# Attention with two mixture layers on one core: maxima and subtractions first, a new start, gate constants in groups, chained weight decodes

## The chip, the core and the metric

The kernel runs on one core of a Trainium2 chip. A core has engines with queues of their own: TensorE (PE) multiplies matrices into PSUM banks, VectorE (DVE), ScalarE (ACT) and GpSimd (POOL) work on elements, SyncE (SP) issues most of the DMA transfers. Each engine runs its queue in order; an instruction that waits holds everything behind it on that engine. What is compared is the time of one launch in microseconds (us); lower is better.

## The reference

```
phi(x) = concat(exp(p), exp(-p)),  p = x @ w_phi - max|x @ w_phi|       # 64 -> 2 x 128 features
kv = phi(k)^T v;  z = sum phi(k)                                        # per batch and head
att = (phi(q) kv) / (phi(q) z + 1e-6)                                   # 8 batches, 8 heads, 576 tokens, 64
x = att as 4608 tokens x 512
h = x @ w_in;  x = (h * cos(h)) @ w_out                                 # first layer, 512 -> 2048 -> 512, float64 weights
logits = x @ w_gate + bias[modality]                                    # second layer: one of 8 experts for a token
out = gate * relu(x @ w1[e]) @ w2[e]                                    # 512 -> 1024 -> 512
```

## The kernel before

**Attention** goes by items: 16 of them, each two batches by two heads. An item's 576 tokens a batch are cut into five groups (`GR`: 2, 2, 1, 2 and 2 chunks), and the program has five steps m=0..4 per item, the one of m=2 with half the work. A step has two halves. `turns(j,m)` (L225) turns a part of the k and q of item j+1 with PE transposes (`pt`), which ACT copies to `kT` and `qT`; turns and exponentiates q features of two steps ago (`ptt`, ACT to `qx`); turns finished outputs (`po`, ACT to `xo`); and lets ACT exponentiate k features (`ke`). `products(j,m)` (L237) puts the projections of q and k into one PSUM tile `pj` (L124), the numerators of item j-1 into `pn` (L198), and `kv` (L162) of two steps ago. DVE then takes, for q and k, the maximum of absolute values (`m_q`, `m_k`, L129) and subtracts it (`t_q`, `t_k`, L130), and divides the numerators (`rd`, `xs`, L203 to L205). `pj` has one buffer (`bufs=1`), so the next step's `pj` starts when `t_k` of this step has read the last one. Nearly all of this is kept in program order.

**Decodes.** The weights of the first layer come as float64. Each of 32 pieces (512 KB) is loaded to a staging tile `st`, and `decoding` (L387) turns it into a pair of float32r tiles: Abs on ACT (L414), `min`, shift, two ORs on DVE (L415 to L418), a cast on ACT (L419), and a subtraction on POOL. In attention there is one staging tile (`sx`); `stage()` asks for the next load right after the second OR and the cast have been issued. The caller of `moes` walks attention by `next(att)`, two a step, and from n=32 on puts one of a decode's four parts (Abs and `min`; shift; first OR; second OR, cast, the next load and the subtraction) at every second n, from n%10==2 of an item; there are 12 such decodes (items 3 to 14), and more during the last 20 of the 170 half steps. The rest is decoded in the first steps of the first layer, one a step.

**Start.** The first k loads, then w_phi, then q and v loads of item 0, then the loads of item 1; five turns ahead of the first `pj`. After 15 half steps `gate_consts` (L266) issues the constants of the second layer's gate and of its routing in one lump, POOL fills a table and a block of zeros, and SP writes them.

**First layer** (`step(F)`): 9 blocks of 512 tokens by 16 pieces; L455 is its first matmul `ph`, and at F>=3 each step decodes one piece as long as any is left.

Of the kernel before, what the change touches and what calls it, by code (L numbers as in the profile page):

```python
# [264 lines left out]

def gate_consts(tc, ctx, cpool, ps, ident, modality_id, modality_bias, w_gate, wgt):  # L266
    nc=tc.nc
    C={}
    with tc.tile_pool(name="g_tmp",bufs=1) as tp:

        wgr=tp.tile([P,4,8],F32,name="wgr")
        nc.sync.dma_start(wgr,w_gate.rearrange("(c p) e -> p c e",p=P))
        pg=ps.tile([P,512],F32,tag="tr",name="pg")
        for c in range(4): nc.tensor.transpose(pg[0:8,c*P:(c+1)*P],wgr[:,c,:],ident)
        gt=tp.tile([8,512],F32,name="gt")
        nc.vector.tensor_copy(gt,pg[0:8,:])
        nc.sync.dma_start(wgt[:,:],gt)
        g1=cpool.tile([P,4,16],F32R,name="g1"); g2=cpool.tile([P,4,16],F32R,name="g2")
        nc.vector.tensor_copy(g1[:,:,0:8],wgr)
        nc.vector.tensor_tensor(g1[:,:,8:16],wgr,f32(g1[:,:,0:8]),ALU.subtract)  # L280
        nc.vector.tensor_copy(g2[:,:,0:8],wgr)
        nc.vector.memset(f32(g2[:,:,8:16]),0.0)

        fold=cpool.tile([16,8],F32,name="fold")
        nc.vector.tensor_tensor(fold,ident[0:16,0:8],ident[0:16,8:16],ALU.add)

        tf=tp.tile([P,P],F32,name="tf")
        nc.gpsimd.memset(tf,1.0)
        nc.gpsimd.affine_select(out=tf,in_=tf,compare_op=ALU.is_gt,fill=0.0,base=0,pattern=[[1,P]],channel_multiplier=-1)
        tri=cpool.tile([P,P],BF16,name="tri"); nc.vector.tensor_copy(tri,tf)  # L290
        one=cpool.tile([P,P],BF16,name="one"); nc.vector.memset(one,1.0)

        ri=tp.tile([P,8],I32,name="ri"); nc.gpsimd.iota(ri,pattern=[[-1,8]],base=8,channel_multiplier=0)
        rev=cpool.tile([P,8],F32,name="rev"); nc.vector.tensor_copy(rev,ri)

        rg=tp.tile([P,8],I32,name="rg"); nc.gpsimd.iota(rg,pattern=[[REG,8]],base=0,channel_multiplier=0)
        run=cpool.tile([P,8],F32,name="run0"); nc.vector.tensor_copy(run,rg)
        base=cpool.tile([P,8],F32,name="base"); nc.vector.tensor_copy(base,rg)
        nm=tp.tile([P,8],I32,name="nm"); nc.gpsimd.iota(nm,pattern=[[1,8]],base=0,channel_multiplier=0)
        num=cpool.tile([P,8],F32,name="num"); nc.vector.tensor_copy(num,nm)  # L300

        sl=tp.tile([1,25],I32,name="sl"); nc.gpsimd.iota(sl,pattern=[[1,25]],base=0,channel_multiplier=0)
        slot=cpool.tile([1,25],F32,name="slot"); nc.vector.tensor_copy(slot,sl)
        ones=cpool.tile([1,16],F32,name="ones"); nc.vector.memset(ones,1.0)

        tok=cpool.tile([P,4,9],I32,name="tok")
        nc.gpsimd.iota(tok[:,:,0:4],pattern=[[1152,4],[1,4]],base=0,channel_multiplier=4)
        nc.gpsimd.iota(tok[0:64,:,4:5],pattern=[[1152,4],[0,1]],base=512,channel_multiplier=1)
        nc.gpsimd.iota(tok[64:128,:,4:5],pattern=[[1152,4],[0,1]],base=1088,channel_multiplier=1)
        nc.gpsimd.iota(tok[:,:,5:9],pattern=[[1152,4],[1,4]],base=576,channel_multiplier=4)  # L310

        mi=tp.tile([P,4,9,2],I32,name="mi")
        ms=modality_id.bitcast(I32).rearrange("(a t w) -> a t w",a=4,w=2)
        for b,c0 in ((0,0),(1,5)):
            nc.sync.dma_start(mi[:,:,c0:c0+4,:].rearrange("p a c w -> p a (c w)"),ms[:,576*b:576*b+512,:].rearrange("a (p c) w -> p a (c w)",c=4))
            nc.sync.dma_start(mi[64*b:64*b+64,:,4,:],ms[:,576*b+512:576*b+576,:].rearrange("a p w -> p a w"))
        mf=tp.tile([P,36],F32,name="mf"); nc.vector.tensor_copy(mf,mi[:,:,:,0].rearrange("p a c -> p (a c)"))
        mz=tp.tile([P,36],F32,name="mz"); nc.vector.tensor_scalar(mz,mf,-1.0,1.0,op0=ALU.mult,op1=ALU.add)
        mb=tp.tile([P,2,8],F32,name="mb")
        nc.sync.dma_start(mb.rearrange("p a e -> p (a e)"),modality_bias.rearrange("(o a) e -> o (a e)",o=1).to_broadcast([P,16]))  # L320
        bt=cpool.tile([P,36,8],F32,name="bt"); b0=tp.tile([P,36,8],F32,name="b0")
        nc.vector.tensor_tensor(bt,mf.unsqueeze(2).to_broadcast([P,36,8]),mb[:,1:2,:].to_broadcast([P,36,8]),ALU.mult)
        nc.vector.tensor_tensor(b0,mz.unsqueeze(2).to_broadcast([P,36,8]),mb[:,0:1,:].to_broadcast([P,36,8]),ALU.mult)
        nc.vector.tensor_tensor(bt,bt,b0,ALU.add)
    C.update(g1=g1,g2=g2,fold=fold,tri=tri,one=one,rev=rev,run=run,base=base,tok=tok,bt=bt,num=num,slot=slot,ones=ones,pool=cpool)
    return C
# [597 lines left out]
def kernel(  # L924
# [28 lines left out]
    def consts():  # L953
        with tc.tile_pool(name="fill", bufs=1) as tp:
# [10 lines left out]
        return gate_consts(tc, ctx, cpool, ps, ident, modality_id, modality_bias, w_gate, wgt)

# [39 lines left out]
```

## Time and profile before

| | |
|---|---|
| time, median of 3 runs | 1710.75 us (1710.69 to 1710.86) |
| the profiled execution | 1708.39 us, span 1706.3 us |
| granted PE clock, mean | 0.987 of full speed |
| busy: PE, weight loads, DVE, ACT, POOL | 95%, 81%, 67%, 49%, 25% |
| attention, first to last `pj` | 11.96 to 373.73 us |

The span runs from the first to the last instruction of the profiled execution; the time is that of the whole launch. Attention ends near 400 us, the first layer near 1200 us, the rest is the second layer.

### The profile page before, as it was taken

Reading aid. Unit: us, or ns where it says so; the run is one execution under the profiler, and the core shown is the slowest. Engines: PE = TensorE matmul, PEld = TensorE weight load, DVE = VectorE, ACT = ScalarE, POOL = GpSimd, SP = SyncE. Lnnn points to the kernel's source line nnn. Section 1 sums busy time; section 2 is a strip of 40 time slices with the busy share of each in tenths; the row PEclk is TensorE's granted clock in tenths of the full one; section 3 lists DMA queues with packets and bytes.
Section 4 is the critical chain, followed back from the end, with each engine's and each line's share of the span. In section 5 each row is a group of like instructions: output and inputs, shape, how many; then the busy total and the mean of one; then the engine's idle time right before and its main releaser. Section 6 shows DMA issues by size and latency. Waiting matters only on the chain.

```text
span 1706.3 us, 33457 instructions
## 1 busy us (share of the span) xinstructions
PE 1618.9 (95%) x13058; PEld 1384.3 (81%) x13058; DVE 1145.9 (67%) x2332; ACT 829.2 (49%) x1529; POOL 427.7 (25%) x351
## 2 busy tenths in 40 slices
PE   6999999989899999999999999999789999999987
PEld 5888888877678888888888888888679999999976
DVE  4677777787885868676777777754556565665545
ACT  4566666655443434343433334343445555655545
POOL 0000000023232433334333333343222112211111
PEclk8999999999999999999999999999899999999999
DMA  6344444423220101010000101001378666767656
GB/s 186 100 134 126 129 137 135 128 91 121 87 99 13 38 13 37 13 37 14 26 25 7 43 7 38 7 7 36 126 240 305 218 219 228 252 210 224 226 167 205
DMA packets 142544, 190.05 MB, mean 111 GB/s; under 512 B 64536, under 2 KB 89240, under 8 KB 142371
## 3 DMA queue, kind: packets, MB, share of 16 engines
q1 hardware_dynamic: 134578, 166.74, 31.0%
q0 software_dynamic: 7792, 21.02, 3.7%
q8 instruction: 107, 1.75, 0.4%
q14 instruction: 67, 0.54, 0.1%
HBM read 157.98 MB, written 30.51 MB: 110 GB/s over the span
## 4 chain that ended last, share of the span: by engine, by line
PE 72%; DVE 13%; issue 5%; DMA 5%; ACT 4%; SPq 1%; POOL 1%; another core or an unknown queue 0%; DVEq 0%; POOLq 0%; ACTq 0%
PE ph L455 19%; PE acc L489 15%; PE mh L739 11%; PE po L751 10%; PE acc L494 4%; PE pj L124 3%; PE kv L162 3%; PE pn L198 2%; DMA tab<-rec,pi 2%; PE pt L109 2%; DVE x L445 1%; DMA raw<-in_moe_w_dram 1%; DVE t_k L130 1%; DVE d_t L406 1%; DVE m_k L129 1%
## 5 line engine op out<-in xcount | busy, mean ns | idle before, releaser
L455 PE MATMUL ph<-x,w 128*128 128x512 f32 x1728 | 424.8, 393 | 9.0 <-DVE fr L475 4.5
L455 PEld LDWEIGHTS ph<-x,w 128*128 128x128 f32 x1728 | 322.7, 188 | 85.7 <-DVE fr L475 7.4
L478 POOL TENSOR_TENSOR gl<-fr,gh 128x512 fp32r<-128x512 f32 x144 | 217.9, 1515 | 437.3 <-DVE gh L477 378.9
L699 DVE TENSOR_TENSOR m<-raw,m 128x512 fp32r<-128x512 f32 x320 | 210.2, 694 | 142.8 <-ACT m L698 142.7
L489 PE MATMUL acc<-w,gh 128*128 128x512 f32 x896 | 276.9, 390 | 1.0 <-DVE w L410 0.6
L698 ACT CAST m<-raw 128x512 fp32r<-128x512 f32 x320 | 187.0, 618 | 68.0 <-PE mh L739 33.6
L739 PEld LDWEIGHTS mh<-xT,m 128*128 128x128 f32 x1728 | 211.2, 193 | 6.3 <-DVE hl L742 2.8
L739 PE MATMUL mh<-xT,m 128*128 128x256 f32 x1728 | 212.3, 284 | 4.0 <-DVE hl L742 2.6
L468 ACT ACTIVATE n<-ph 128x512 int32<-128x512 f32 x144 | 85.8, 596 | 256.3 <-PE ph L455 256.2
L489 PEld LDWEIGHTS acc<-w,gh 128*128 128x128 f32 x896 | 168.2, 188 | 37.5 <-DVE w L410 1.9
L470 DVE SCALAR_TENSOR_TENSOR fr<-ph,n 128x512 f32<-128x512 f32 x144 | 99.2, 689 | 141.7 <-ACT n L468 127.9
L519 DVE SCALAR_TENSOR_TENSOR junk<-x1T,wg 128x512 f32<-128x512 f32 x224 | 183.3, 818 | 0.0
L751 PE MATMUL po<-m,hh 128*128 128x512 f32 x576 | 180.1, 394 | 1.8 <-ACT hh L741 1.8
L489 PE MATMUL acc<-w,gl 128*128 128x512 f32 x448 | 174.4, 389 | 0.0
L472 ACT ACTIVATE fr<-fr 128x512 f32<-128x512 f32 x144 | 91.1, 633 | 153.1 <-DVE fr L470 152.3
L475 DVE SCALAR_TENSOR_TENSOR fr<-fr,ph 128x512 f32<-128x512 f32 x144 | 98.7, 685 | 68.5 <-ACT fr L473 68.4
L751 PEld LDWEIGHTS po<-m,hh 128*128 128x128 f32 x576 | 105.3, 188 | 22.0 <-ACT hh L741 2.3
...
L751 PE MATMUL po<-m,hl 128*128 128x512 f32 x288 | 112.4, 390 | 0.1
L129 DVE TENSOR_REDUCE m_q<-pj 128x4 f32<-128x512 f32 (+1 forms) x80 | 51.0, 638 | 84.6 <-PE pj L124 84.5
L489 PEld LDWEIGHTS acc<-w,gl 128*128 128x128 f32 x448 | 84.1, 188 | 17.4
L473 ACT ACTIVATE fr<-fr 128x512 f32<-128x512 f32 x144 | 91.0, 632 | 4.3
(195 smaller groups left out, 2365.0 us busy)
## 6 DMA issues: line engine op xcount, KB each, us to landing
...
```

The costliest lines, as they stand in the source:

```text
L455: nc.tensor.matmul(ph,A[:,ws],xhl[u,d][k],start=n[0]==0,stop=n[0]==11); n[0]+=1
L470: nc.vector.scalar_tensor_tensor(g,ph,INV2PI,n,op0=ALU.mult,op1=ALU.subtract)
L472: nc.scalar.activation(g,g,AF.Sin,scale=math.pi)
L473: nc.scalar.activation(g,g,AF.Square)
L475: nc.vector.scalar_tensor_tensor(g,g,-0.5,ph,op0=ALU.add,op1=ALU.mult)
L478: nc.gpsimd.tensor_tensor(gl,g,f32(gh),ALU.subtract)
L489: nc.tensor.matmul(accs[u][c],A[:,ws],B,start=(f==0 and k==0),stop=(f==NF-1 and k==2))
L519: return lambda: tc.keep_in_program_order(nc.vector.scalar_tensor_tensor(junk,x1T[u,c],1.0,wg[e],op0=ALU.mult,op1=ALU.mult,accum_out=lgs[u ...
L698: keep(nc.scalar.copy(h,a))
L699: keep(nc.vector.tensor_tensor(l,a,f32(h),ALU.subtract))
L739: nc.tensor.matmul(ph[:,f2*T:(f2+1)*T],A[:,ws],B[d//2][:,xs],start=n==0,stop=n==11); n+=1
L751: nc.tensor.matmul(po[c],A[:,ws],B,start=(f==0 and j==0),stop=(f==NF2-1 and j==2))
```

## The change

In each step DVE takes both maxima and both subtractions before it divides the numerators, and the 64-wide `kv` of m=4 is issued behind `pj` instead of ahead of it. The first loads are k and q of both batches, then w_phi, then the small remainders; only the turns of m=0 and m=3 stand ahead of the first `pj`, and the others are spread by `FIRST`. Matmuls on a tile of zeros (`warm`) are put at the start (6) and in the steps of item 0 (3). `gate_consts` is a generator whose groups come at n=9, 17, 19, 21, 23 and 25. The stepped decodes become 14; they are chained, so that the last part of one and the first of the next come in one call, and a part is taken at four of the ten half steps of an item, from n=10. Two more tiles take decoded weights during attention (`xw`, 6 for 4), two fewer later (`wl`, 12 for 14).

```diff
-    ld("k",0)
-    for s in range(2): nc.sync.dma_start(w2[s*D:(s+1)*D,:],w_phi)
-    ld("q",0); ld("v",0)
+    load_first()
+    ld("v",0)
     for t in "kqv": ld(t,1)
-    for m in range(5): turn(0,m)()
+    warm(6)
+    for m in (0,3): turn(0,m)()
...
+    FIRST=((),((0,2),),((0,1),(0,4)),((1,0),(1,1)),((1,2),(1,3)))
...
-        for n in ((),(0,),(1,),(2,3),(4,))[m] if j==0 else (m,) if j+1<NI else (): vecs.append(turn(j+1,n))
+        for i,n in FIRST[m] if j==0 else ((1,4),(2,0)) if j==1 and m==0 else ((j+1,m),):
+            if i<NI: vecs.append(turn(i,n))
...
+        vecs=proj(j,m) if j<NI else []
         if todo and g==2: kv(i,g)
-        vq=vk=vn=None
-        if j<NI: vq,vk=proj(j,m)
-        if 0<=j-1<NI: vn=num(j-1,m)
+        if 0<=j-1<NI: vecs.append(num(j-1,m))
+        elif m<4: warm(3)
         if todo and g!=2: kv(i,g)
-        if vq: vq()
-        if vn: vn()
+        for f in vecs: f()
         if todo and g==2: kvfin(i,0)
         if todo and g==4: kvfin(i,1)
-        if vk: vk()
...
-    for _ in range(15): next(att)
-    C=consts()
-    stage()
-    for n in range(15,170-TAIL):
+    setup=consts()
+    work=itertools.chain.from_iterable(decoding(steps=True) for _ in range(14))
+    for n in range(170-TAIL):
         next(att)
-
-        if n%10==2 and 3<=n//10<15: work=decoding(steps=True)
-        if n>=32 and n%2==0: next(work,None)
+        if n==8: stage()
+        if n==9: next(setup)
+        if n in (17,19,21,23): C=next(setup)
+        if n==25:
+            for _ in setup: pass
+        if 10<=n and n%10 in (0,2,4,6): next(work,None)
+    for _ in work: pass
...
-    early=["wx"]*5+["qe"]*3+["xw"]*4+["xT"]*4+["raw_q","sx"]
+    early=["wx"]*5+["qe"]*3+["xw"]*6+["xT"]*4+["raw_q","sx"]
```

How the engines' queues change is shown at three places. The number in a name such as `m_q_1` is the step m; the last number only tells tiles apart.

DVE, a step m=1 of a middle item, in the kernel before (L415 is the `min` of a decode, L416 its shift, L168 copies `kv` to `kvz`):

```order
L129 TENSOR_REDUCE m_q_1_1771<-pj_1_1726 128x4
L130 TENSOR_TENSOR t_q_1_1731<-pj_1_1726,m_q_1_1771 128x512
L415 TENSOR_SCALAR d_t_1_1722<-d_t_1_1722 128x512
L203 TENSOR_SCALAR rd_1_1774<-pn_1_1737 128x4
L129 TENSOR_REDUCE m_k_1_1780<-pj_1_1726 128x4
L204 RECIPROCAL rd_1_1774<-rd_1_1774 128x4
L168 COPY kvz_1_1778<-kv_1_1562 128x260
L205 TENSOR_TENSOR xs_1_1754<-pn_1_1737,rd_1_1774 128x256
L130 TENSOR_TENSOR t_k_1_1736<-pj_1_1726,m_k_1_1780 128x512
L416 TENSOR_SCALAR d_t_1_1722<-d_t_1_1722 128x512
```

Here `t_k` stands behind the division and the copy. DVE, the same step in the changed kernel, from the last operation of one decode (L435, the second OR) to the `min` (L432) and shift (L433) of the next:

```order
L435 SCALAR_TENSOR_TENSOR d_t_2_1068<-st_0_1065,d_t_2_1068 128x512
L141 TENSOR_REDUCE m_q_1_1428<-pj_1_1383 128x4
L142 TENSOR_TENSOR t_q_1_1388<-pj_1_1383,m_q_1_1428 128x512
L141 TENSOR_REDUCE m_k_1_1431<-pj_1_1383 128x4
L215 TENSOR_SCALAR rd_1_1434<-pn_1_1394 128x4
L142 TENSOR_TENSOR t_k_1_1393<-pj_1_1383,m_k_1_1431 128x512
L216 RECIPROCAL rd_1_1434<-rd_1_1434 128x4
L180 COPY kvz_1_1438<-kv_1_1224 128x260
L432 TENSOR_SCALAR d_t_3_1379<-d_t_3_1379 128x512
L217 TENSOR_TENSOR xs_1_1411<-pn_1_1394,rd_1_1434 128x256
L433 TENSOR_SCALAR d_t_3_1379<-d_t_3_1379 128x512
```

`t_k` now stands ahead of the division's last steps and of the copy, and the next decode's `min` follows the last decode's second OR by one step. ACT in the kernel before, where a decode begins: its Abs (L414) stands behind the exponentials of a step, far from the cast (L419) of the decode before, two steps and more earlier:

```order
L419 CAST w_0_1326<-d_t_0_1325 128x512
L112 COPY kT_1612<-pt_0_1611 128x512
L183 ACTIVATE qx_3_1622<-ptt_3_1617 128x2x256 x2
L216 COPY xo_1396<-po_3_1623 128x256
L141 ACTIVATE ke_4_1630<-t_k_4_1580 128x4x128
L142 ACTIVATE ke_4_1630<-t_k_4_1580 128x4x128
L112 COPY kT_1612<-pt_1_1688 128x512
L183 ACTIVATE qx_4_1698<-ptt_4_1693 128x2x256 x2
L216 COPY xo_1396<-po_4_1699 128x256
L141 ACTIVATE ke_0_1707<-t_k_0_1643 128x4x128
L142 ACTIVATE ke_0_1707<-t_k_0_1643 128x4x128
L414 ACTIVATE d_t_1_1722<-st_0_1558 128x512
```

The same place on ACT in the changed kernel (L436 the cast, L431 the next Abs, L124 copies of turned k and q):

```order
L153 ACTIVATE ke_0_1359<-t_k_0_1295 128x4x128
L154 ACTIVATE ke_0_1359<-t_k_0_1295 128x4x128
L436 CAST w_2_1069<-d_t_2_1068 128x512
L431 ACTIVATE d_t_3_1379<-st_0_1376 128x512
L124 COPY kT_1263<-pt_2_1440 128x128
L124 COPY qT_1442<-pt_2_1440 128x128
L195 ACTIVATE qx_0_1449<-ptt_0_1444 128x2x256 x2
L228 COPY xo_1450<-po_0_1451 128x256
```

The Abs now stands right behind the cast, and the copies of the next turn behind the Abs. Last, DVE where item 1 begins, in the kernel before (`rev` and `run` are constants from POOL):

```order
L129 TENSOR_REDUCE m_k_4_361<-pj_4_345 128x4
L130 TENSOR_TENSOR t_k_4_355<-pj_4_345,m_k_4_361 128x512
L129 TENSOR_REDUCE m_q_0_427<-pj_0_382 128x4
L294 CAST rev<-ri 128x8
L297 CAST run_602<-rg 128x8
L130 TENSOR_TENSOR t_q_0_387<-pj_0_382,m_q_0_427 128x512
```

and in the changed kernel (`mf` is a cast of the loaded modality numbers `mi`):

```order
L141 TENSOR_REDUCE m_k_4_380<-pj_4_357 128x4
L180 COPY kvz_0_383<-kv_0_250 128x260
L142 TENSOR_TENSOR t_k_4_367<-pj_4_357,m_k_4_380 128x512
L286 CAST mf<-mi 128x36
L286 TENSOR_SCALAR mz<-mf 128x36
L141 TENSOR_REDUCE m_q_0_497<-pj_0_452 128x4
L432 TENSOR_SCALAR d_t_0_448<-d_t_0_448 128x512
L142 TENSOR_TENSOR t_q_0_457<-pj_0_452,m_q_0_497 128x512
```

`rev` and `run` stand ahead of the first step of all now; `mf` and `mz` stand ahead of `m_q` of item 1, and the first decode's `min` behind it.

## Rows read from the trace of the kernel before

**Rows 1.** Busy time of each engine, 200 to 220 us: us and instructions, clock, DMA share.

```profile
200.00:220.00 20.00, 17.95 (x352) 16.15 (x351) 14.68 (x37) 14.32 (x33) 1.41 (x2) 1.00 0.49 147
```

**Rows 2.** Waits, 60 to 340 us: engine, waiting line, releaser: total, times, longest.

```profile
PE pj L124 <- DVE t_k L130: 24.6, 25, 1.3
```

**Rows 3.** Timeline, PE: start, us, line, operation, tiles, in brackets the idle before.

```profile
200.29 0.71 PE L124 MATMUL pj<-w,qT 64*128 64x128 f32 x8
...
205.80 0.49 PE L124 MATMUL pj<-w,qT 64*128 64x128 f32 x4 [1.31 <-DVE t_k L130]
...
209.24 0.71 PE L124 MATMUL pj<-w,qT 64*128 64x128 f32 x8
...
213.26 1.11 PE L162 MATMUL kv<-v,ke 64*128 64x65 f32 x16
214.21 0.67 PE L124 MATMUL pj<-w,qT 64*128 64x128 f32 x8
...
218.39 0.72 PE L124 MATMUL pj<-w,qT 64*128 64x128 f32 x8 [0.74 <-DVE t_k L130]
...
222.74 0.71 PE L124 MATMUL pj<-w,qT 64*128 64x128 f32 x8
```

**Rows 4.** Timeline, DVE, steps m=4 and m=0 of the same item.

```profile
217.55 0.69 DVE L130 TENSOR_TENSOR t_k<-pj,m_k 128x512 f32<-128x512 f32 x1
...
219.59 0.69 DVE L129 TENSOR_REDUCE m_q<-pj 128x4 f32<-128x512 f32 x1 [1.01 <-PE pj L124]
```

**Rows 5.** Groups of DVE by shape, 60 to 340 us: busy, mean ns, idle before.

```profile
L129 DVE TENSOR_REDUCE m_q<-pj 128x2 f32<-128x256 f32 x12 | 5.1, 425 | 7.1 <-PE pj L124 7.1
```

**Rows 6.** The staging tile, 60 to 340 us; one decode's load, Abs and `min`.

```profile
DMA to landing us min/median/max: 3.7/4.7/6.3
...
214.25 0.34 SPq L380 DMA_DIRECT2D st<-in_moe_w_out_dram  x1
...
224.94 0.70 ACT L414 ACTIVATE d_t<-st 128x512 f32<-128x512 f32 x1
...
225.68 0.43 DVE L415 TENSOR_SCALAR d_t<-d_t 128x512 f32<-128x512 f32 x1 [0.32 <-ACT d_t L414]
```

**Rows 7.** Timeline of the start: PE, DVE and SP.

```profile
34.28 0.72 PE L124 MATMUL pj<-w,qT 64*128 64x128 f32 x8 [1.97 <-DVE t_k L130]
...
35.37 1.95 PE L198 MATMUL pn<-kvz,qx 128*64 128x65 f32 x32
...
42.36 1.22 PE L124 MATMUL pj<-w,qT 64*128 64x128 f32 x8 [2.30 <-DVE g L279]
...
61.97 0.71 PE L124 MATMUL pj<-w,qT 64*128 64x128 f32 x8 [0.75 <-DVE t_k L130]
...
39.55 0.17 DVE L294 CAST rev<-ri 128x8 f32<-128x8 int32 x1 [3.38 <-POOL ri L293]
...
43.67 0.18 DVE L317 CAST mf<-mi 128x36 f32<-128x36 int32 x1 [0.97 <-DMA mi<-in_moe_modality_id_dram]
...
39.57 0.50 SPq L315 DMA_DIRECT2D mi<-in_moe_modality_id_dram  x1
```

**Rows 8.** Timeline, PE, the last `pj` and a wait behind it.

```profile
373.73 0.67 PE L124 MATMUL pj<-w,qT 64*128 64x128 f32 x8
...
387.13 0.50 PE L455 MATMUL ph<-x,w 128*128 128x512 f32 x1 [1.54 <-DVE x L446]
```

**Rows 9.** Timeline, PE, first layer: steps F=15 to 17 and the next.

```profile
469.28 3.06 PE L455 MATMUL ph<-x,w 128*128 128x512 f32 x12 [1.08 <-DVE fr L475]
...
477.42 0.73 PE L455 MATMUL ph<-x,w 128*128 128x512 f32 x2 [1.14 <-DVE x L445]
...
486.69 2.88 PE L455 MATMUL ph<-x,w 128*128 128x512 f32 x12
...
492.27 2.88 PE L455 MATMUL ph<-x,w 128*128 128x512 f32 x12
```

More of the change, by code (lines that the diff above doesn't have):

```diff
@@ L79, in load_v, with load_first @@
         return r
+    def load_first():
+        rs={}
+        for t,src in (("k",k),("q",q)):
+            rs[t]=S("raw_"+t,f"raw_{t}_0").rearrange("p (h c d) -> p h c d",h=2,d=D), raw.tile([P,2,D],F32,tag="rl_"+t,name=f"rl_{t}_0")
+        for bb in range(2):
+            for t,src in (("k",k),("q",q)):
+                nc.sync.dma_start(rs[t][0][:,:,4*bb:4*bb+4,:].rearrange("p h c d -> p h (c d)"), src[bb,0:2,0:512,:].rearrange("h (p c) d -> p h (c d)",c=4))
+        for s in range(2): nc.sync.dma_start(w2[s*D:(s+1)*D,:],w_phi)
+        for bb in range(2):
+            for t,src in (("k",k),("q",q)): nc.sync.dma_start(rs[t][1][64*bb:64*bb+64,:,:], src[bb,0:2,512:576,:].rearrange("h p d -> p h d"))
+        for t in "kq": raws[t,0]=rs[t]
     raws={}
@@ L240, in products, with warm @@
         todo=0<=i<NI
+        vecs=proj(j,m) if j<NI else []
         if todo and g==2: kv(i,g)
-        vq=vk=vn=None
-        if j<NI: vq,vk=proj(j,m)
-        if 0<=j-1<NI: vn=num(j-1,m)
+        if 0<=j-1<NI: vecs.append(num(j-1,m))
+        elif m<4: warm(3)
         if todo and g!=2: kv(i,g)
-        if vq: vq()
-        if vn: vn()
+        for f in vecs: f()
         if todo and g==2: kvfin(i,0)
         if todo and g==4: kvfin(i,1)
-        if vk: vk()
         if j==NI-1 and m==4: pctx.close()
-    ld("k",0)
-    for s in range(2): nc.sync.dma_start(w2[s*D:(s+1)*D,:],w_phi)
-    ld("q",0); ld("v",0)
+    zb=ap.tile([P,512],BF16,name="zb",bufs=1)
+    nc.vector.memset(zb,0.0)
+    def warm(n):
+        pw=ps.tile([P,512],F32,tag="nm",name="warm")
+        for i in range(n): keep(nc.tensor.matmul(pw,zb[:,0:P],zb,start=i==0,stop=i==n-1))
+    load_first()
+    ld("v",0)
     for t in "kqv": ld(t,1)
-    for m in range(5): turn(0,m)()
+    warm(6)
+    for m in (0,3): turn(0,m)()
     for j in range(NI+1):
@@ L263, in attention, with gate_consts @@
     for m in range(2): turns(NI+1,m)
-def gate_consts(tc, ctx, cpool, ps, ident, modality_id, modality_bias, w_gate, wgt):
+def gate_consts(tc, ctx, cpool, ps, ident, modality_id, modality_bias, w_gate, wgt, tp):
     nc=tc.nc
[L268 to L326, printed above, removed]
@@ new lines, in gate_consts @@
+    keep=tc.keep_in_program_order
+    V=lambda op,*a,**k: keep(getattr(nc.vector,op)(*a,**k))
+    wgr=tp.tile([P,4,8],F32,name="wgr")
+    nc.sync.dma_start(wgr,w_gate.rearrange("(c p) e -> p c e",p=P))
+    mi=tp.tile([P,4,9,2],I32,name="mi")
+    ms=modality_id.bitcast(I32).rearrange("(a t w) -> a t w",a=4,w=2)
+    for b,c0 in ((0,0),(1,5)):
+        nc.sync.dma_start(mi[:,:,c0:c0+4,:].rearrange("p a c w -> p a (c w)"),ms[:,576*b:576*b+512,:].rearrange("a (p c) w -> p a (c w)",c=4))
+        nc.sync.dma_start(mi[64*b:64*b+64,:,4,:],ms[:,576*b+512:576*b+576,:].rearrange("a p w -> p a w"))
@@ new lines, in gate_consts @@
+    mb=tp.tile([P,2,8],F32,name="mb")
+    nc.sync.dma_start(mb.rearrange("p a e -> p (a e)"),modality_bias.rearrange("(o a) e -> o (a e)",o=1).to_broadcast([P,16]))
+    tf=tp.tile([P,P],F32,name="tf")
+    nc.gpsimd.memset(tf,1.0)
+    nc.gpsimd.affine_select(out=tf,in_=tf,compare_op=ALU.is_gt,fill=0.0,base=0,pattern=[[1,P]],channel_multiplier=-1)
+    ri=tp.tile([P,8],I32,name="ri"); nc.gpsimd.iota(ri,pattern=[[-1,8]],base=8,channel_multiplier=0)
+    rg=tp.tile([P,8],I32,name="rg"); nc.gpsimd.iota(rg,pattern=[[REG,8]],base=0,channel_multiplier=0)
@@ new lines, in gate_consts @@
+    nm=tp.tile([P,8],I32,name="nm"); nc.gpsimd.iota(nm,pattern=[[1,8]],base=0,channel_multiplier=0)
+    sl=tp.tile([1,25],I32,name="sl"); nc.gpsimd.iota(sl,pattern=[[1,25]],base=0,channel_multiplier=0)
+    tok=cpool.tile([P,4,9],I32,name="tok")
+    nc.gpsimd.iota(tok[:,:,0:4],pattern=[[1152,4],[1,4]],base=0,channel_multiplier=4)
+    nc.gpsimd.iota(tok[0:64,:,4:5],pattern=[[1152,4],[0,1]],base=512,channel_multiplier=1)
+    nc.gpsimd.iota(tok[64:128,:,4:5],pattern=[[1152,4],[0,1]],base=1088,channel_multiplier=1)
@@ new lines, in gate_consts @@
+    nc.gpsimd.iota(tok[:,:,5:9],pattern=[[1152,4],[1,4]],base=576,channel_multiplier=4)
+    yield
+    pg=ps.tile([P,512],F32,tag="tr",name="pg")
+    for c in range(4): keep(nc.tensor.transpose(pg[0:8,c*P:(c+1)*P],wgr[:,c,:],ident))
+    g1=cpool.tile([P,4,16],F32R,name="g1"); g2=cpool.tile([P,4,16],F32R,name="g2")
+    V("tensor_copy",g1[:,:,0:8],wgr)
+    V("tensor_tensor",g1[:,:,8:16],wgr,f32(g1[:,:,0:8]),ALU.subtract)
+    V("tensor_copy",g2[:,:,0:8],wgr)
+    gt=tp.tile([8,512],F32,name="gt")
@@ new lines, in gate_consts @@
+    V("tensor_copy",gt,pg[0:8,:])
+    nc.sync.dma_start(wgt[:,:],gt)
+    yield
+    nc.vector.memset(f32(g2[:,:,8:16]),0.0)
+    fold=cpool.tile([16,8],F32,name="fold")
+    V("tensor_tensor",fold,ident[0:16,0:8],ident[0:16,8:16],ALU.add)
+    tri=cpool.tile([P,P],BF16,name="tri"); V("tensor_copy",tri,tf)
+    one=cpool.tile([P,P],BF16,name="one"); nc.vector.memset(one,1.0)
+    rev=cpool.tile([P,8],F32,name="rev"); V("tensor_copy",rev,ri)
+    run=cpool.tile([P,8],F32,name="run0"); V("tensor_copy",run,rg)
@@ new lines, in gate_consts @@
+    base=cpool.tile([P,8],F32,name="base"); V("tensor_copy",base,rg)
+    yield
+    num=cpool.tile([P,8],F32,name="num"); V("tensor_copy",num,nm)
+    slot=cpool.tile([1,25],F32,name="slot"); V("tensor_copy",slot,sl)
+    ones=cpool.tile([1,16],F32,name="ones"); nc.vector.memset(ones,1.0)
+    mf=tp.tile([P,36],F32,name="mf"); V("tensor_copy",mf,mi[:,:,:,0].rearrange("p a c -> p (a c)"))
+    mz=tp.tile([P,36],F32,name="mz"); V("tensor_scalar",mz,mf,-1.0,1.0,op0=ALU.mult,op1=ALU.add)
+    yield
@@ L329, in moes @@
+    bt=cpool.tile([P,36,8],F32,name="bt"); b0=tp.tile([P,36,8],F32,name="b0")
+    V("tensor_tensor",bt,mf.unsqueeze(2).to_broadcast([P,36,8]),mb[:,1:2,:].to_broadcast([P,36,8]),ALU.mult)
+    V("tensor_tensor",b0,mz.unsqueeze(2).to_broadcast([P,36,8]),mb[:,0:1,:].to_broadcast([P,36,8]),ALU.mult)
+    V("tensor_tensor",bt,bt,b0,ALU.add)
+    yield dict(g1=g1,g2=g2,fold=fold,tri=tri,one=one,rev=rev,run=run,base=base,tok=tok,bt=bt,num=num,slot=slot,ones=ones,pool=cpool)
 def moes(tc, ctx, consts, S, ps, ident, att, end_att, xt, w_in, w_out, x1d, tab, wgt, w1, w2, out):
@@ L344, in pair @@
     def pair(tag,name):
-        if tag=="wl": t=late[0].tile([P,1024],F32R,tag="wl",name=name,bufs=14)
+        if tag=="wl": t=late[0].tile([P,1024],F32R,tag="wl",name=name,bufs=12)
         else: t=S(tag,name,F32R)
@@ L359, in stg @@
         n=turns.get("stg",0)
-        return S(turn(("sx",)*12+("raw_k",)*5 if n<17 else ("raw_k","raw_k","raw_q"),"stg"),name,I32)
+        return S(turn(("sx",)*14+("raw_k",)*5 if n<19 else ("raw_k","raw_k","raw_q"),"stg"),name,I32)
     seq=[(0,0),(1,0)]
@@ L393, in decoding @@
         H=v[:,:,1]; L=v[:,:,0]
-        t=xtile("gl" if decoded[0]<=17 else "row",f"d_t{which}_{f}",F32)
+        t=xtile("gl" if decoded[0]<=19 else "row",f"d_t{which}_{f}",F32)
         ti=t.bitcast(I32)
@@ L675, in alloc_w @@
             tag=wtag[1][n]
-            t=late[0].tile([P,1024],F32,tag="wl",name=f"raw_{n}",bufs=14) if tag=="wl" else S(tag,f"raw_{n}",F32)
+            t=late[0].tile([P,1024],F32,tag="wl",name=f"raw_{n}",bufs=12) if tag=="wl" else S(tag,f"raw_{n}",F32)
             RAW.append(t[:,0:1024])
@@ L964, in consts @@
                 nc.sync.dma_start(x1d[LAST + c * P : LAST + (c + 1) * P, :], zero)
[L965 removed]
+            yield from gate_consts(tc, ctx, cpool, ps, ident, modality_id, modality_bias, w_gate, wgt, tp)
     S, ps = shared_tiles(tc, ctx)
```

2 lines of the change are left out of this document (1 added, 1 removed).

## The prediction

> **What bounds the kernel now.** I read the row of engine busy times for 20 us of mid-attention first, since every part of the change but one lies in the first 400 us. There TensorE (PE) works 17.95 of 20 us and VectorE (DVE) 14.68, at full clock, 2.4 GHz [rows 1]. No engine is full, so the waits decide: between 60 and 340 us PE waits 25 times, 24.6 us in all, for `t_k` before it may write the next projection `pj` [rows 2]. `pj` has a single buffer: the next one waits until DVE has read both halves of the present one.
>
> The timeline of PE gives one item as five steps, pj to pj [rows 3]. From the row at 200.29 to that at 222.74 an item takes 22.45 us, of which 1.31 and 0.74 are waits for `t_k`. So PE's own spacing is 4.20 (m=1 to 2), 3.44, 4.97, 3.44 (4.18 less the wait) and 4.35: 20.40 us. If DVE is never late, that is the pitch.
>
> DVE's ring [rows 3, 4]: `pj` starts at 218.39 and `m_q` at 219.59, 1.20 later. The `t_k` that ended at 218.24 (217.55 and 0.69) let that `pj` go, 0.15 later. (Steps are written as item and step below: `pj`(1,0) is the first projection of item 1.)
>
> **The change part by part.**
>
> *Maxima and subtractions first.* `m_q`, `t_q`, `m_k`, `t_k` follow each other at about 0.69 each: 2.75 us. The ring of a full step becomes 1.20 + 2.75 + 0.15 = 4.10, that of the half step m=2 some 0.76 + 1.75 + 0.15 = 2.66, with 0.42 for each of its four [rows 5]. The three operations for `xs` now lie beside PE's `pn`, `kv` and transposes instead of in the ring. PE's spacing must exceed the ring in every step: 4.20, 3.44 and 4.35 do, 3.44 (m=4 to 0) would not. For that the 64-wide `kv` (16 matmuls, 213.26 to 214.21, 0.95, [rows 3]) moves behind `pj` of m=4: 4.97 becomes 4.02, 3.44 becomes 4.39. The first is then 0.08 short of 4.10, so I take 20.5 an item. Without any decode 13 items would take 13 x 20.5 = 266.5, and item 15, which turns nothing ahead and so goes at DVE's ring, 3 x 4.10 + 3.0 = 15.3 to its last `pj`: 281.8 us from the first `pj` of item 2 to the last of item 15. Before, 61.97 to 373.73 were 311.76 [rows 7, 8]. So the gain is at most 30.0.
>
> *The chained decodes take most of it back.* A stepped decode asks for its successor's 512 KB load after its last DVE operation has read the staging tile (one buffer). Before, the next Abs on ScalarE (ACT) stood at a fixed place of the next item; the load at 214.25 was needed at 224.94, 10.7 us later, and DVE waited 0.32 for each Abs [rows 6]. Now the Abs is queued on ACT right behind the cast of the one before, and the first DVE step of the new decode, a `min`, stands among the projections of the next step, in program order. Such a load takes 3.7 / 4.7 / 6.3 us (least, median, most) to land, and Abs to `min` 0.74 (224.94 to 225.68) [rows 6]. From the end of the last OR to the `min` that is 0.1 + 4.7 + 0.74 = 5.5 us, little more than one step, and everything behind the waiting `min` on DVE waits too, then PE for `t_k`.
>
> The order repeats every 3 items with 4 decodes. Case A: last OR after `xs` at m=0, `min` at m=1 after `kvz`. With `pj`(m=0) at 0, `t_k` ends at 3.95, `xs` and the OR (0.68) at 5.0; landing 9.75, Abs to 10.5. `min` would have gone at 8.65; `xs` and the shift follow, `m_q` of m=2 starts at 11.55, and 1.75 + 0.15 later `pj`(m=3) may start: 13.45 against PE's 12.0. Lost: 1.45. ACT holds the next turn's copies behind that Abs as well; by the same sum they let `pj`(m=3) go at 13.05, so DVE is last. In the same way B (OR at m=4, `min` at m=0 after `t_k`) loses 1.5, C (m=2 to m=3, the load behind the v loads on SP) 1.7, D (m=1 to m=3, between `m_k` and `t_k`) 2.0, and the second decode to the third 2.7. Over the 12 handovers of items 2 to 13: 3 x 1.45 + 3 x 1.5 + 3 x 1.7 + 2 x 2.0 + 2.7 = 20.65. Two of the six later decodes, which now start in items 13 and 14, add 2.96 and 0.85: 3.8. So 281.8 + 20.65 + 3.8 = 306.2, a gain of 5.6, between 30 (every load in time) and -13.6 (each at the most of [rows 6], 1.6 later, 12 x 1.6).
>
> The Trainium skill says (DMA: Bandwidth & Descriptors, Rules for kernel authors) that a load should be issued early and its semaphore waited on late. This chain does the opposite: it issues 5 us ahead of the need, where the kernel before left 10.7. The trace agrees that the distance of before was enough.
>
> *Start.* The first loads put k and q ahead, and two turns instead of five stand ahead of the first `pj`: I take `pj`(0,0) 3.6 us earlier, and `pj`(1,0), with the rings of item 0 shorter too, at 29.7 for 34.28. But DVE now meets `mf`, which needs the gate's `mi` load, ahead of `m_q` of item 1. Before, `mf` ran at 43.67, 4.1 us after the first `mi` issue at 39.57; now that issue stands behind the loads and table writes on SP, around 31.1, and `mf` runs near 35.2. So `m_q`(1,0) starts near 35.6, as late as before (1.20 after 34.28). What goes is the stall of 3.38 on `rev`; PE's idle of 2.30, and the projection at half the clock after it (1.22 for 0.71), go too [rows 7]. The first decode's handover then loses about 1.5. `pj`(2,0) comes at 60.0 for 61.97: +2.0, between 0 and 8.9 (29.7 + 20.5 + 2 x 1.5 = 53.1, if `mf` is in time).
>
> *Clock.* Ahead of the `pj` at 34.28 PE was idle for 1.97 us, and the `pn` behind it took 1.95; after an idle of 2.30 `pj` took 1.22 for 0.71 [rows 3, 7]: 1.2 GHz, half the rate, for about two groups of matmuls, which costs some 1.6 (my estimate: a `pn` and as much again at twice their time). After an idle of 1.31 the half-size `pj` of 205.80 took 0.49, less than the 0.71 of a whole one [rows 3]. The stalls of 2.0 and more lie beyond the first, A to C between the two. I take 2.5 drops: -4.0; bounds 0 and 14 x 1.6 = -22.4.
>
> *Hand-over and MoE1.* At 387.13 PE waits 1.54 for an x whose DVE queue stood behind a tail decode [rows 8]; that decode is gone from there: +1.5 (0 to 1.5). MoE1 decodes 12 weights in its first steps instead of 14: the steps at F=15 and 16 took 8.14 (469.28 to 477.42) and 9.27 (to 486.69) for the 5.58 of the next, without a decode (to 492.27) [rows 9]: 6.25 in excess, of which I leave 0.75 to the start of a block, which has work of its own: +5.5 (4.0 to 6.3). The six warm-up matmuls and three a step in item 0 lie in PE's idle there: nothing.
>
> Sum: 2.0 + 5.6 - 4.0 + 1.5 + 5.5 = +10.6. The profiled run took 1708.39 (span 1706.3), 2.4 under the median; from it I get 1697.8, and on the median 1700.
>
> **The rivals.**
>
> *The loads land in time.* If a load lands at the least of [rows 6], 3.7 instead of 4.7, each handover loses 1.0 less: A 0.45, B 0.5, C 0.7, D 1.0, the first 1.7, in all 8.7 with the start of the later ones 2; the clock never falls. Gain 2.0 + (30.0 - 10.7) + 7.0 = 28: 1682. For it: the chip's DMA engines are half idle there (0.49, [rows 1]); against it: the median of 13 such loads was taken in the same half-idle stretch. The Trainium skill's fit (DMA: Bandwidth & Descriptors, Anatomy of one DMA, the SWDGE path) is 2.0 us plus bytes over 436,000 a us: 3.2 for 512 KB, and by it my estimate would be 1675. The trace's least, on SP's queue, is 3.7: the fit, taken on another path, is short here. Chance 0.2, with 1670 at the far end, where also `mf` is in time.
>
> *Slower: the clock falls at each stall.* If an idle of 1.45 us already halves PE's clock, the 14 stalls cost 22.4 instead of 4.0: gain -7.8, 1718.5. It decides from a loss of 1.6 at 10 stalls on. If loads also land at 5.5, 1728. For it: A, B and C lie between 1.31 without and 1.97 with a fall. Against: A and B, six of the twelve, lie nearer to 1.31. Chance 0.17.
>
> *No difference.* Loads that land 0.7 later than the median, behind the v loads, cost 12 x 0.7 = 8.4 and the gain is 2: 1708.5. Chance 0.11.
>
> **How the numbers follow.** Forecast, between 1690 and 1706, 0.52; in time 0.2; slower 0.17; no difference 0.11. Faster by more than 0.2% (3.4 us, about what a measurement of this kernel tells from none) holds the first two, 0.72. The range of 1670 to 1719 leaves out about 0.05 below and 0.12 above.
>
> **What would show it.** Right: in the waits of 60 to 340 us PE for `t_k` falls from 25 to some 14 entries, most over 1.3 us, and DVE's `min` waits on ACT's Abs, Abs on the load, 1.5 us and more a time; spans of items without a handover are 20.4 to 20.5; `rev` has no stall, and `mf` one for `mi` of some 4 us. A pitch of 22 in items without a handover would refute the ring; a `min` that hardly waits, the chain's cost; a granted clock below 0.95 in mid-attention, the small clock term. The step I trust least is the 4.7.

## The result: slower, and where the time went

The changed kernel takes 1726.91 us (median of 8 runs, 1718.06 to 1733.34), the kernel before 1710.74 in the same runs: a ratio of 1.0095, interval 1.0072 to 1.0118. The forecast was 1700. The profiled execution has a span of 1723.9 us, 17.6 above that of before. The runs of the changed kernel differ by 15 us, those of before by 7, and a likely reason, which no run shows by itself, is that its time hangs on how fast single loads land.

The timeline of PE gives the stretches. First, the first `pj` of items 2, 12 and 13 and the last of item 15 (start, duration, line, operation):

```profile
66.55 0.71 PE L136 MATMUL pj<-w,qT 64*128 64x128 f32 x8
...
306.30 0.72 PE L136 MATMUL pj<-w,qT 64*128 64x128 f32 x8
...
326.79 0.71 PE L136 MATMUL pj<-w,qT 64*128 64x128 f32 x8
...
388.56 0.71 PE L136 MATMUL pj<-w,qT 64*128 64x128 f32 x8 [0.51 <-DVE rd L216]
```

Item 12, which hands no decode over, takes 20.49 us for the 22.45 of before: the new step order does what was forecast. Every other stretch but the last falls short of its forecast. Against before, stretch by stretch (us, + is slower; before from [rows 7 to 9] and the same timeline):

| stretch | forecast | measured |
|---|---|---|
| to `pj`(2,0) | -2.0 | +4.6 (66.55 for 61.97) |
| `pj`(2,0) to `pj`(12,0), with the clock | +5.9 | +16.0 (239.75 for 223.76) |
| `pj`(12,0) to `pj`(15,4) | -7.4 | -5.7 |
| `pj`(15,4) to step F=4 of the first layer | -1.5 | -1.2 |
| F=4 to F=19 | -5.5 | +3.9 (98.60 for 94.70) |
| rest | 0 | 0 |

The waits of the changed kernel between 60 and 340 us (total, times, longest) answer to [rows 2]:

```profile
ACT d_t L431 <- DMA st<-in_moe_w_in_dram: 25.9, 7, 5.6
DVE d_t L432 <- ACT d_t L431: 25.1, 12, 4.7
PE pn L210 <- DVE xs L217: 16.5, 8, 5.1
...
PE pj L136 <- DVE rd L215: 3.8, 3, 2.9
PE pj L136 <- DVE t_k L142: 3.6, 2, 2.3
```

Of the 24.6 us for `t_k` 8.8 are left, in the two rows of `pj` and a third of 1.4. (The profile names `rd` for some of them. `rd` stands right beside `t_k` on DVE, but `pj` needs nothing of the division: what it waits for is still that `t_k` has read the last `pj`.) In place of the rest a chain of waits runs through three engines: Abs on ACT waits for the load, `min` on DVE waits for Abs (12 times, once per handover), PE waits for what stands behind `min` on DVE. And PE waits mostly at `pn`, not at `pj`. The worst handover shows it, in time order on SP, ACT, DVE and PE:

```profile
238.42 0.88 SPq L66 DMA_DIRECT2D raw_k<-in_k_dram  x2
239.53 0.37 SPq L395 DMA_DIRECT2D st<-in_moe_w_in_dram  x1
...
247.41 0.66 ACT L431 ACTIVATE d_t<-st 128x512 f32<-128x512 f32 x1 [5.59 <-DMA st<-in_moe_w_in_dram]
...
248.10 0.43 DVE L432 TENSOR_SCALAR d_t<-d_t 128x512 f32<-128x512 f32 x1 [4.71 <-ACT d_t L431]
248.44 0.42 DVE L217 TENSOR_TENSOR xs<-pn,rd 128x256 f32<-128x256 f32 x1
...
249.01 1.13 PE L210 MATMUL pn<-kvz,qx 128*64 128x65 f32 x16 [5.15 <-DVE xs L217]
249.90 1.98 PE L174 MATMUL kv<-v,ke 128*64 128x65 f32 x32
251.81 1.12 PE L121 MATMUL pt<-ident,raw_q 128*128 128x128 f32 x4
```

The staging load is asked for 1.1 us behind two loads of k and is used 7.9 us later (239.53 to 247.41). `xs` of m=1 stands behind the `min` on DVE. It reads a bank that `pn` of m=2 needs (there are two, and `po` has the other), so PE stops 5.15 us at `pn`, with only `pj` of the step done, and then runs `kv` and `pt` at half the rate (1.98 and 1.12; `kv` is 1.10 elsewhere). The clock row of 220 to 260 us answers to [rows 1], with 0.87 for 1.00:

```profile
220.00:260.00 40.00, 32.38 (x570) 29.55 (x565) 24.14 (x59) 21.14 (x49) 2.62 (x3) 0.87 0.39 108
```

At the start DVE meets `mf`, and later the second decode's Abs holds ACT (rows of DVE, PE, ACT and PE), against [rows 7]:

```profile
36.19 0.18 DVE L286 CAST mf<-mi 128x36 f32<-128x36 int32 x1 [7.79 <-DMA mi<-in_moe_modality_id_dram]
...
39.59 1.23 PE L136 MATMUL pj<-w,qT 64*128 64x128 f32 x8 [6.93 <-DVE rd L216]
...
56.31 0.66 ACT L431 ACTIVATE d_t<-st 128x512 f32<-128x512 f32 x1 [4.05 <-DMA st<-in_moe_w_in_dram]
...
58.02 0.69 PE L189 MATMUL ptt<-ident,t_q 128*128 128x128 f32 x2 [3.89 <-ACT qT L124]
```

In the first layer the block boundary at F=16 answers to [rows 9]. It takes 14.42 us (490.10 to 504.52) where it took 9.27:

```profile
490.10 0.73 PE L472 MATMUL ph<-x,w 128*128 128x512 f32 x2 [1.42 <-DVE x L462]
493.52 1.22 PE L472 MATMUL ph<-x,w 128*128 128x512 f32 x2 [2.68 <-DVE x L462]
495.54 1.22 PE L472 MATMUL ph<-x,w 128*128 128x512 f32 x2 [0.79 <-DVE x L462]
497.77 2.93 PE L472 MATMUL ph<-x,w 128*128 128x512 f32 x6 [1.02 <-DVE x L462]
504.52 2.89 PE L472 MATMUL ph<-x,w 128*128 128x512 f32 x12
```

PE waits four times for a cast of the next block's x (L462). On DVE these casts now stand apart, between the parts of the last decode (L422, L423, L427) and of `fr`:

```profile
490.30 1.76 DVE L422 SCALAR_TENSOR_TENSOR d_t<-st,d_t 128x512 int32<-128x512 int32 x1
491.98 1.48 DVE L462 CAST x<-xr 128x512 fp32r<-128x512 f32 x1
493.39 0.68 DVE L423 SCALAR_TENSOR_TENSOR d_t<-st,d_t 128x512 int32<-128x512 int32 x1
493.99 1.49 DVE L462 CAST x<-xr 128x512 fp32r<-128x512 f32 x1
495.40 0.68 DVE L487 SCALAR_TENSOR_TENSOR fr<-ph,n 128x512 f32<-128x512 f32 x1
496.00 1.38 DVE L427 TENSOR_TENSOR w<-d_t,w 128x512 fp32r<-128x512 f32 x1
497.30 0.41 DVE L462 CAST x<-xr 128x512 fp32r<-128x512 f32 x1
```

In the kernel before, the last three of the four casts followed each other without anything between:

```profile
477.89 3.24 DVE L445 CAST x<-xr 128x512 fp32r<-128x512 f32 x3
```

### The profile page after: what moved, and what is told of

It is laid out like the page before. It is cut to its first block, busy times and chain, and to the rows that moved or that the text cites. A ratio compares the mean times of both kernels' runs of the same rounds, so it can differ in the third digit from the quotient of the medians.

```text
span 1723.9 us, 33528 instructions
## 1 busy us (share of the span) xinstructions
PE 1635.5 (95%) x13076; PEld 1397.7 (81%) x13076; DVE 1148.1 (67%) x2331; ACT 828.2 (48%) x1529; POOL 428.6 (25%) x353
## 4 chain that ended last, share of the span: by engine, by line
PE 72%; DVE 12%; DMA 8%; ACT 3%; issue 3%; SPq 1%; POOL 1%; DVEq 0%; POOLq 0%; ACTq 0%
PE ph L472 19%; PE acc L506 14%; PE mh L756 11%; PE po L768 10%; PE acc L511 4%; PE pj L136 3%; DMA st<-in_moe_w_in_dram 3%; PE pn L210 3%; PE kv L174 2%; DMA tab<-rec,pi 1%; DMA st<-in_moe_w_out_dram 1%; DVE x L462 1%; PE pt L121 1%; DMA raw<-in_moe_w_dram 1%; DVE d_t L423 1%
## 5 line engine op out<-in xcount | busy, mean ns | idle before, releaser
L489 ACT ACTIVATE fr<-fr 128x512 f32<-128x512 f32 x144 | 91.1, 633 | 153.6 <-DVE fr L487 153.0
L210 PE MATMUL pn<-kvz,qx 128*64 128x65 f32 x2304 | 90.2, 233 | 18.7 <-DVE xs L217 16.5
L210 PEld LDWEIGHTS pn<-kvz,qx 128*64 128x64 f32 x2304 | 79.5, 145 | 29.5 <-issue 16.5
```

Source lines behind the costliest of these rows:

```text
L210: keep(nc.tensor.matmul(o[64*c:64*c+64],x[:,h,sg,t*P+64*c:t*P+64*c+64],kvs[i,bb][:,2*h+sg,:],start=sg==0,stop=sg==1,skip_group_check=True))
L489: nc.scalar.activation(g,g,AF.Sin,scale=math.pi)
```

## The experiments

Times are medians; the kernel before had 1710.55 in the runs of the first four, 1711.15 in those of the next four and 1711.44 in the last two.

**One decode per item, not chained.** Theory 1 is that the chain costs; the rival, that the new step order does.

```diff
-    work=itertools.chain.from_iterable(decoding(steps=True) for _ in range(14))
...
-        if 10<=n and n%10 in (0,2,4,6): next(work,None)
+        if n%10==2 and 1<=n//10<15: work=decoding(steps=True)
+        if n%2==0: next(work,None)
```

> The changed kernel with one decode per item (items 1 to 14, a part at each second half step from m=1), not chained; all else as changed, 14 decodes too. Theory 1 (the chain costs: each load is asked for some 5 us before its min): the stalls of 33 us between pj(2,0) and pj(12,0) go, the pitch is 20.5, and the time about 1684. Rival (the new order in a step costs: xs behind both subtractions holds the bank that pn needs, whatever the decodes do): PE still waits for xs at pn, the pitch stays at 22 or more, and the time above 1708. With theory 1 the stall for mf at the start (7.8 us) stays, and so does the slow block boundary of the first layer.

Measured 1694.83, ratio 0.9899 (0.9876 to 0.9922). The waits, 60 to 340 us:

```profile
PE pj L136 <- DVE rd L216: 10.3, 15, 1.2
...
DVE d_t L432 <- ACT d_t L431: 4.1, 13, 0.3
```

The `min` hardly waits, PE never waits at `pn`. That is 32 us below the changed kernel from the order of the decodes alone, with the same 14 decodes: theory 1 holds. The order changes two things at once, how early a load is asked for (9.8 us ahead of its Abs, for 3.5 to 7.9 when chained) and where the `min` stands; the run with two staging tiles parts them. The time is 11 above the expected 1684; some 8 of that is the pitch, 21.1 for 20.5, as 0.6 us of the ring are left at m=1, and the rest is not traced. The Trainium skill's rule (DMA: Bandwidth & Descriptors, Rules for kernel authors) is to issue a load early and wait for it late; this run agrees with it: between 60 and 340 us no Abs waits for a load.

**The new step order alone**, put into the kernel before.

```diff
-        if todo and g==2: kv(i,g)
-        vq=vk=vn=None
-        if j<NI: vq,vk=proj(j,m)
-        if 0<=j-1<NI: vn=num(j-1,m)
+        vecs=proj(j,m) if j<NI else []
+        if todo and g==2: kv(i,g)
+        if 0<=j-1<NI: vecs.append(num(j-1,m))
         if todo and g!=2: kv(i,g)
-        if vq: vq()
-        if vn: vn()
+        for f in vecs: f()
...
-        if vk: vk()
```

> The kernel before with the new order in a step alone (both maxima and subtractions ahead of the division, the 64-wide kv behind pj), its 12 unchained decodes, start and constants as before. Theory 1: pitch 20.4 to 20.5 for 22.4, time about 1684, with the block boundary of the first layer as before. Rival: within 5 us of 1710.7.

Measured 1690.44, ratio 0.9874 (0.985 to 0.9898). The step order gains 20 us; pitch 21.10 (`pj`(3,0) at 82.17, `pj`(12,0) at 272.05) for 22.45. So the rest of the change cost 36 us, across two sets of runs.

**`mf` and `mz` moved to the last group of constants** in the changed kernel (their two lines stand ahead of `bt`).

> The changed kernel with the two operations on the modality numbers (mf, mz) in the last group of constants, beside those that use them, and so not ahead of m_q of item 1. If the 7.8 us stall on mf delays all that follows, pj(1,1) comes near 33 instead of 39.6 and pj(2,0) 6 us earlier, time about 1720. If the next load of a decode then is the limit (it is asked for by program order, not by time), 2 us or less: 1725.

Measured 1730.14 (1720.81 to 1734.54), ratio 1.0092 (1.006 to 1.0124): no gain. `pj`(1,1) does come 3.9 earlier and `pj`(2,0) 4.4 (PE and ACT rows):

```profile
35.69 0.71 PE L136 MATMUL pj<-w,qT 64*128 64x128 f32 x8 [2.09 <-DVE rd L216]
...
52.87 0.66 ACT L431 ACTIVATE d_t<-st 128x512 f32<-128x512 f32 x1 [5.80 <-DMA st<-in_moe_w_in_dram]
...
62.19 0.71 PE L136 MATMUL pj<-w,qT 64*128 64x128 f32 x8
```

But the second decode's Abs then waits 5.80 for 4.05, and `pj`(12,0) is at 307.40 for 306.30. This profile is of the slowest of the five runs, and the runs of either kernel spread over 14 to 15 us. So whether the time won at the start is waited for at later loads, or is hidden by that spread, stays open.

**Two staging tiles**, the chain kept, each load asked for one decode earlier.

```diff
-"sx":(1024,1)
+"sx":(1024,2)
...
-        if n==8: stage()
+        if n==8: stage(); stage()
```

> The changed kernel, chained as it is, with two staging tiles and the loads asked for one decode earlier (about 20 us ahead instead of 5). One more decoded tile early and one less late pays for the space. Theory 1 in its narrow form (the load is late, not the place of the min on DVE): no min waits for a load, the pitch is 20.5, time about 1690. Rival (the place of min, shift and ORs among the projections costs by itself): 1715 or more.

Measured 1706.06, ratio 0.9968 (0.9952 to 0.9984): 21 below the changed kernel, 16 above the narrow theory. Between the two: loads are in time, yet PE still waits. The rows of ACT, DVE, PE and POOL at one handover:

```profile
174.38 0.72 ACT L431 ACTIVATE d_t<-st 128x512 f32<-128x512 f32 x1
...
175.13 1.03 DVE L432 TENSOR_SCALAR d_t<-d_t 128x512 f32<-128x512 f32 x1 [0.81 <-ACT d_t L431]
...
177.62 0.71 PE L136 MATMUL pj<-w,qT 64*128 64x128 f32 x8 [1.28 <-DVE rd L216]
...
174.58 1.28 POOL L428 TENSOR_TENSOR w<-d_t,w 128x512 fp32r<-128x512 f32 x1 [18.04 <-ACT w L436]
```

Here the Abs waited for no load. It ran when ACT had finished the cast ahead of it, and the `min`, 1.84 with its wait, stands between `t_q` and `m_k`, in the ring. So the place of the `min` is a cost of its own. Part of it is a longer `min`: it takes 1.00 to 1.09 at every handover of this run, beside POOL's subtraction of the decode before (the last row), and 0.43 at every one of the changed kernel, where it comes later than that subtraction. From `pj`(2,0) to `pj`(12,0) this kernel loses 22.6 us above ten pitches of 20.49, the changed one 34.9.

**The new start**, with `mf` late, on the new step order with 12 unchained decodes and the tiles of before.

> The kernel of the run with the new step order alone, plus the new start (loads, turns, constants in groups, with mf and mz in the last group): 12 unchained decodes in items 3 to 14, tiles as before, so the first layer decodes 14 as before. If the new start is worth what the traces of the changed kernel and of the run with mf late show (pj(1,0) 4.9 us earlier, no idle for rev or mf), pj(2,0) comes at 52 to 55 and the time is 1681 to 1684. Rival: the start's gain is eaten by other loads, within 2 us of 1690.4.

Measured 1681.75, ratio 0.983 (0.9799 to 0.9861). `pj`(2,0) comes at 51.20, 10.5 earlier than with the step order alone, and 8.7 of that are left at the end.

**The first layer's decodes at F=5 to 16**, on the unchained kernel with 14.

```diff
-            if F>=3 and decoded[0]<2*NF: decode(True)
+            if F>=5 and decoded[0]<2*NF: decode(True)
```

> The changed kernel unchained (14 decodes, one per item), and the first layer's 12 decodes at F=5 to 16 instead of 3 to 14, so that the last falls where it fell before. If the boundary's 14.4 us (against 9.3) come from the last decode's ORs standing between the casts of the next block, the boundary is 9 to 10 us again and the time 1690 for 1694.8. Rival (12 or 14 decodes, wherever they stand, cost the same at the boundary): 1694.8.

Measured 1691.1, ratio 0.9885 (0.9855 to 0.9916); 3.7 less than unchained alone, across two sets of runs. The boundary itself is clear:

```profile
456.10 0.73 PE L472 MATMUL ph<-x,w 128*128 128x512 f32 x2 [1.16 <-DVE x L462]
458.11 1.51 PE L472 MATMUL ph<-x,w 128*128 128x512 f32 x4 [1.28 <-DVE x L462]
459.87 2.73 PE L472 MATMUL ph<-x,w 128*128 128x512 f32 x6 [0.24 <-DVE x L462]
465.38 2.88 PE L472 MATMUL ph<-x,w 128*128 128x512 f32 x12
```

9.28 us (456.10 to 465.38) for about 14.2 in the unchained run: with the same number of decodes it is where the last one falls, not how many there are.

**Parts of a decode one half step later**, on the step order alone.

```diff
-        if n%10==2 and 3<=n//10<15: work=decoding(steps=True)
-        if n>=32 and n%2==0: next(work,None)
+        if n%10==3 and 3<=n//10<15: work=decoding(steps=True)
+        if n>=32 and n%2==1: next(work,None)
```

> The kernel of the run with the new step order alone, with the parts of a decode one half step later (behind the products of a step, so that the min no longer stands between t_q and m_k of m=1). If the 0.6 us that pitch 21.1 is above 20.5 is that min in the ring, the pitch falls to 20.4 to 20.5, PE waits for the division no more, and the time is 1683. Rival: the other parts take its place in the ring, 1690.

Measured 1684.54, ratio 0.9844 (0.9811 to 0.9878), 5.9 below. The pitch is 20.58 (81.99 to 267.18), and of the 14 waits of `pj` on DVE that the step order alone had (put down to `rd`, as above), 3 are left:

```profile
PE pj L124 <- DVE rd L204: 2.9, 3, 1.4
```

**All four mends** on the changed kernel.

> The changed kernel with the four mends together: unchained decodes (14), their parts one half step later, mf and mz late, first layer's decodes at F=5 to 16. If the terms add: start 6, pitch 0.6 x 14, boundary 5 below the unchained run: about 1676. If the first layer again takes back what 14 early decodes give: 1680 or more.

Measured 1679.93, ratio 0.9805 (0.977 to 0.984). That interval, 1672 to 1684 us, holds the 1676 of added terms and the rival's 1680 alike, so this run does not decide.

**The mends with 12 decodes.**

> The new step order, the new start with mf late, 12 unchained decodes with their parts one half step later: the two gains that the last runs showed apart (start -9, parts later -6) added to 1690.4. If they add: 1676. If 14 decodes in attention are worth more than the work they add there, this is slower than the run with all four mends (1679.9); if not, it is faster.

Measured 1676.7, ratio 0.9789 (0.9764 to 0.9814), the fastest of all: the gains of start and place add. The interval overlaps that of 14 decodes, so which number is better stays open. PE is now busy 239.14 of 240 us (columns as in [rows 1]), at full clock:

```profile
60.00:300.00 240.00, 239.14 (x4735) 217.31 (x4737) 200.70 (x480) 168.99 (x385) 15.22 (x22) 1.00 0.48 138
```

**No k and q loads from item 2 on**, in the changed kernel: items 2 to 15 use the k and q of items 0 and 1, so the outputs and the routing are others.

```diff
+        if t!="v" and 2<=i<NI: raws[t,i]=raws[t,i-2]
+        elif i<NI: raws[t,i]=load_v(i) if t=="v" else load(t,{"k":k,"q":q}[t],i)
```

> The changed kernel, chained, with the k and q loads of items 2 to 15 left out (these items use the k and q of items 0 and 1 again). In the changed kernel the staging loads of case A, asked for 1.1 us behind the two raw_k loads, took 5.6, 5.8 and 7.9 us to their Abs; those of case B 3.5 to 3.7. If the k loads beside them make them late: all land in 3.5 to 4.3, A loses some 1.5 as the prediction had it, and the time is about 1712. Rival (A's loads are all of w_in, rows of 1 KB, and late for that): A's stay at 5.6 and more, and the time is within 5 us of 1727.

Measured 1727.01, which says nothing here: with other routing the second layer takes 537.2 us (last `ph` to the end) for 520.4. Attention itself ends 14.5 us earlier (`pj`(15,4) at 374.02 for 388.56). The same handover as the worst one above (SP, ACT, PE):

```profile
227.96 0.38 SPq L396 DMA_DIRECT2D st<-in_moe_w_in_dram  x1
...
232.19 0.66 ACT L432 ACTIVATE d_t<-st 128x512 f32<-128x512 f32 x1 [1.97 <-DMA st<-in_moe_w_in_dram]
...
234.18 1.13 PE L211 MATMUL pn<-kvz,qx 128*64 128x65 f32 x16 [1.92 <-DVE xs L218]
```

4.2 us from issue to Abs for 7.9; the other two of case A take 4.5 for 5.6 and 5.8. So the form of `w_in` does not make case A's loads late, and the k loads ahead of them are part of the cause. An `xt` store and v loads follow A's load in both kernels; whether the k loads would do it without these, no run shows. A still loses 2.3 to 3.5 where I had 1.45: that is the wait at `pn`.

## Why the prediction was wrong

By the table of stretches, of the profiled executions, the time came out 28 us above the forecast's sum: 10.1 of it between `pj`(2,0) and `pj`(12,0), 9.4 in the first layer, 6.6 in the start, 2.0 in the rest.

**The ring: right.** 20.49 for an item without a handover, against 20.5 forecast, and 20 us for the step order alone. The forecast's 30.0 was a bound without any decode; with its 12 decodes the step order alone gained 18.4 from `pj`(2,0) to `pj`(15,4). Some 7 of the difference is the `min` at m=1, which stayed in the ring of every unchained item (0.6 us each); some 4 lies behind `pj`(12,0) and is not traced.

**The chained decodes: the mechanism right, its price wrong.** This is the largest step that failed. I had 20.65 for 12 handovers and 4.0 for the clock. From `pj`(2,0) to `pj`(12,0) the changed kernel lost 34.9 above ten pitches of 20.49, and 33.5 of it at the handovers (which lie in items 2 to 10, not 2 to 13). By case, issue to Abs and what PE lost:

| case | load to Abs, us | lost, us | forecast, us |
|---|---|---|---|
| second to third decode | 4.1 | 5.8 | 2.7 |
| A, three | 5.6, 5.8, 7.9 | 3.2, 3.1, 7.5 | 1.45 each |
| B, three | 3.7, 3.6, 3.5 | 0.6, 0.5, 0.4 | 1.5 each |
| C, three | 4.2, 5.3, 4.0 | 1.5, 4.2, 1.5 | 1.7 each |
| D, two | 4.0, 4.3 | 1.4, 3.8 | 2.0 each |

Case A cost 9.4 more than forecast, B gave back 3.0. The first error was one time for every load. The twelve average 4.7, the very median that I used, but a load's time goes with its place. But ten of the thirteen loads behind that median stood 1.2 to 1.9 us behind two loads of q, 256 KB each. The rows: SP ahead of the load at 214.25 of [rows 6]; landings of those ten, from 100 to 306 us of the kernel before; landings of nine in the run with the parts one half step later, 100 to 285 us, where no load was issued in the 4 us ahead.

```profile
213.04 0.89 SPq L66 DMA_DIRECT2D raw_q<-in_q_dram  x2
...
DMA to landing us min/median/max: 4.2/4.7/6.3
...
DMA to landing us min/median/max: 3.6/3.7/4.2
```

Chained, each load stands at a fixed place among the others: B alone, A behind the k loads and ahead of an `xt` store, C and D behind v loads that also hold SP (1.0 to 2.6 us from the last OR to the issue, where I had 0.1). The second error was to let PE wait at `pj` alone: behind a late `min` stands `xs`, and `pn` waits for its bank a whole step's work earlier. With loads of 4.2 to 4.5, less than I had, case A still lost 2.3 to 3.5. Third, the two staging tiles show that the place of the `min` costs even when the load is there. Fourth, the clock: I had 2.5 falls in all, there were 4 at these handovers and more at the start. The case D with a fall lost 3.8; the other, whose load was there 1.0 sooner after the OR, 1.4. The granted clock of 0.87 in 220 to 260 us is below the 0.95 that I had named as the sign against the small clock term.

**The start: the step failed.** `mf` did wait, 7.79 us where I had some 4 against the time of before: it ran at 36.19, a microsecond later than forecast, and PE paid with an idle of 6.93 and a step at half clock (`pj` 1.23, which I had said would go), then 3.89 us for the second decode. I had put the first handover at 1.5. The upper bound of 8.9 that I gave for `mf` in time was close: the new start gives 10.5 when `mf` and the chain are gone.

**The first layer: the step failed.** I took the two long steps of [rows 9] for the cost of two decodes. They are the boundary of a block, which costs about 9.3 with 14 or with 12 decodes. Two decodes fewer gave 0.9, not 5.5 (F=4 to F=19: 93.80 in the run with decodes at F=5 to 16, 94.70 before), and the place of the last one among the casts cost 5.

**The rivals.** "The loads land in time" was refuted: eight of the twelve took over 4.0 to their Abs. The Trainium skill's fit (DMA: Bandwidth & Descriptors, Anatomy of one DMA), which is given for loads issued by GpSimd, makes 3.2; the least here, on SP's queue, was 3.5. The slower rival named 1718.5, and 1728 with loads at 5.5; the time came out there, but not by its mechanism: the clock fell at 4 of 12 handovers between `pj`(2,0) and `pj`(12,0), not at each. Nor were the loads later on the whole, as its 1728 had it: they averaged 4.7, and only case A and one of C took over 5.
